# Loading k in token order and packing the shift taps two to a pass, in a convolution-plus-MLP kernel

## The chip, the cores and the metric

The kernel runs on one core of one Trainium2 chip. The metric is the device time of one execution in microseconds (us). Executions of one kernel spread by about one per cent, so every comparison below is of several executions, taken in rounds that alternate a kernel with the kernel before on the same chip. A ratio is the mean time of one kernel's fast executions over that of the other's of the same rounds, so it is not quite the ratio of the medians that are quoted. Each run also leaves one profiled execution, from which all times inside the kernel are read; a difference of about 1 us between two profiled executions is within what one kernel shows twice.

Engines: PE multiplies matrices, DVE and ACT are the two engines that move results out of PSUM ("evacuate" them), Pool is a third element-wise engine, SP only issues DMA transfers. A line such as L317 is a line of that run's kernel; the numbers differ from run to run where lines were added.

## The reference, cut to what matters

```python
def _A_ref(q, k, v, shift_k, ssm_k, ssm_D):        # S = 2048 tokens, D = 512 channels
    k_pad = jnp.pad(k, ((0, 0), (ks - 1, 0), (0, 0)))            # ks = 4 taps
    for t in range(ks):
        k_shift = k_shift + k_pad[:, t:t + S, :] * shift_k[:, ks - 1 - t][None, None, :]
    kv = k_shift * v
    y = ...            # long convolution of kv with ssm_k along the tokens, by FFT
    return q * (y + kv * ssm_D)

def _B_ref(x, w1, b1, w2, b2): ...                  # layer norm, w1, gelu, w2
x = A_q
x = x + _A_ref(_layernorm(x), A_k, ...);  x = x + _B_ref(_layernorm(x), ...)
x = x + _A_ref(_layernorm(x), A_k, ...);  x = x + _B_ref(_layernorm(x), ...)
```

The convolution part of A depends on k, v and the filters alone, so it is computed once. The kernel therefore has a *front* (K = transform of the filter, U = transform of kv, X = second stage of U, T = product of X and K, V and Y = the way back) and then an *MLP stretch* of eight groups, in which the PE is never idle.

## The kernel before: the parts that matter

Work is cut into named pieces. A long string, ORDER, gives their order in the program and for each its engine (`P`, `D`, `A`, `G` Pool, `S` sync) and its buffer. Every engine runs its own pieces strictly in that order.

```python
ORDER = """
warm.P dg0.G lK0.S lK1.S lk1.S lk3.S dg3.G KT0.P0 lk0.S KT1.P1 ... lv0.S lx0.S ... lK2.S
lv1.S ... lH.S ... lk2.S ... lK3.S lM.S ... lW.S ... kv30.P1 ... kv00.P2
# ... (cut)
... Y02.P3 ho.G w1.S w2.S V32.P1 ... TP03.P0 TP13.S pc11.A TP23.S TP03e.D ...
... LT0.P3 gb2.A Y10.P1 Y11.P0 LT0e.D Y10e.A ... Y20.P2 ... LT2.P3 m10x0.P1 ...      # m1.. = MLP
"""
    kT = place([P, CT, NT, KC], 80 * K)                   # KC = 128 + 16
    kd = k_d.rearrange("(p nt) d -> nt p d", nt=NT)       # 16 stripes of 128 tokens
    def ktload(q):                                        # each transposes 128 tokens x 512 channels
        def fn(it):
            for i in range(4 * q, 4 * q + 4):
                nc.sync.dma_start_transpose(kT[:, :, i, 16:16 + P], kd[i])
    # ...
        def diag(it, ct=ct):                              # diagonal matrices of the taps, on Pool
            for t in range(KS):
                nc.gpsimd.tensor_scalar(out=DG[:, ct, t, :], in0=IDt[:], scalar1=sF[:, ct, t:t + 1], ...)
    # ...
            def mms(o, cc=cc, o2=o2):                     # kv: taps of channel chunk cc, token half o2
                for i in range(8):
                    for t in range(KS):
                        tau = 8 * o2 + i - t
                        w = kT[:, cc, tau, 16:16 + P] if tau >= 0 else kT[:, cc, tau + NT, 15:15 + P]
                        nc.tensor.matmul(o[:, i, :], w, DG[:, cc, t, :], start=t == 0, stop=t == KS - 1)
            pe = mm(f"kv{cc}{o2}", 1880, [lk[q] for q in ((0, 1, 3) if o2 == 0 else (1, 2, 3))] + [dg[cc]], mms, [8, P])
            # kvm: uv = taps * v, out of PSUM on DVE; first_stage(...) then makes U from uv
```

Dependences of `kv`: a channel chunk needs three of the four groups of k loads, because each load brings all channels of 128 tokens.

## Time and profile before

| | us |
|---|---|
| median of three executions | 274.45 |
| span of the profiled execution | 271.9 |
| first U product on the PE | 26.1 |
| last V evacuation done | 98.4 |
| first MLP matmul | 113.3 |

The first view is the busy time of each engine in three stretches of before (stretch, its length, then busy us and number of instructions for each engine, the granted PE clock, the DMA share, which can pass 1 as the profile counts it, and GB/s).

```profile
core 0: us, PE busy (x) PEld busy (x) DVE busy (x) ACT busy (x) POOL busy (x), PEclk, DMA share, GB/s
0.00:25.00 25.00, 17.97 (x194) 16.26 (x195) 8.46 (x9) 9.82 (x9) 12.29 (x30) 0.89 0.76 176
25.00:50.00 25.00, 22.84 (x286) 20.40 (x284) 19.17 (x27) 12.77 (x13) 1.24 (x2) 0.91 1.13 297
50.00:90.00 40.00, 37.44 (x541) 33.80 (x539) 38.63 (x41) 37.98 (x41) 0.52 (x1) 1.00 1.00 233
```

DVE and ACT are the engines to look at. In the third stretch they are busy 38.6 and 38.0 of 40 us, so little but less evacuation work could shorten it. In the first two they are busy 27.6 and 22.6 of 50 us: here there is time to win.

What they wait for is in the timeline of the sync queue (start, duration of the issue, line, transfer, count).

```profile
1.72 16.80 SPq L340 DMA_TRANSPOSE arena<-in_A_k_dram  x12
18.57 0.58 SPq L296 DMA_DIRECT2D arena<-in_A_v_dram  x1
...
20.14 0.65 SPq L296 DMA_DIRECT2D arena<-in_A_v_dram  x1
...
21.49 8.06 SPq L340 DMA_TRANSPOSE arena<-in_A_k_dram  x4
...
31.48 0.43 SPq L296 DMA_DIRECT2D Wt<-tabW  x1
```

Twelve transposing loads of k occupy the queue for 16.8 us before v is even asked for; the table W is asked for at 31.5 us. The waits that answer to this are in the list of waits (engine, what it was about to do, what released it, total us, times, longest), of DVE and of the PE:

```profile
DVE arena L422 <- DMA arena<-in_A_v_dram: 9.7, 1, 9.7
```

```profile
PE p_91 L417 <- DMA arena<-in_A_k_dram: 4.4, 4, 1.3
...
PE p_91 L387 <- DMA Wt<-tabW: 2.1, 1, 2.1
```

DVE waited 9.7 us for v before its first multiplication with the taps, the PE 4.4 us in four times for k between the taps, and 2.1 us for W.

The tail before the MLP is in the timeline of all engines, cut to the PE and the sync queue. L507 and L524 finish the first group, L576 transposes its layer norm, L533 are the Y products of later groups and L621 is the first MLP matmul.

```profile
97.76 2.71 SPq L490 DMA_DIRECT2D arena<-in_B_w_dram  x1
...
98.45 0.62 PE L507 MATMUL p_90<-IDt,ZT_77 128*128 128x128 bf16 x8 [1.12 <-ACT ZT_77 L476]
...
100.97 3.43 SPq L512 DMA_TRANSPOSE ZT_83<-ZT_77  x1
...
105.78 1.04 PE L576 MATMUL p_93<-IDt,arena 128*128 128x128 bf16 x8 [5.32 <-DVE arena L268]
...
109.02 1.86 PE L533 MATMUL p_91<-ZT_83,GPt 128*128 128x512 bf16 x4 [2.21 <-issue]
...
113.33 0.93 PE L621 MATMUL p_91<-arena 128*128 128x256 bf16 x7
```

The transpose issued at 100.97 us stands behind the three weight loads (the last at 97.76 us) and its own issue is held up for 3.43 us. The Y product at 109.02 us needed it and the PE had been idle for 2.2 us.

### The profile page before, as it was taken

The page shows a single profiled execution, that of the slowest core. Times are in us where ns is not written, and L with a number is a line of the kernel's source. Part 1 is how long each engine was busy: PE and PEld are TensorE (multiplying, and loading weights), DVE is VectorE, ACT ScalarE, POOL GpSimd, SP SyncE. Part 2 cuts the span into 40 slices and gives each one's busy share as a digit, 9 for nine tenths or more (in the row PEclk, how much of TensorE's full clock was granted, in tenths as well). Part 3 has the DMA queues.
Part 4 walks back from the last instruction along what each step waited for, and adds up shares of the span by engine and source line. Part 5 has one row for each costly group of instructions (what it writes and reads, how often), then busy time and mean ns, then how long its engine had stood idle before and what let it go on. Part 6 is the DMA issues. An engine that isn't in the chain of part 4 may idle for free.

```text
span 271.9 us, 4713 instructions
## 1 busy us (share of the span) xinstructions
PE 243.8 (90%) x1880; PEld 152.6 (56%) x1880; DVE 174.0 (64%) x346; ACT 145.8 (54%) x200; POOL 34.8 (13%) x66
## 2 busy tenths in 40 slices
PE   7839996998999541999999999999999999999994
PEld 7729994996898431595444444444444444444441
DVE  0914875998999899499995987977046920030132
ACT  2650665698999862398475346266704287036000
POOL 3950100000000022103203011111001010000000
PEclk9995997999999995799999999999999999999999
DMA  7949999969899999904034021050210131011111
GB/s 193 128 100 366 270 409 197 218 172 220 315 190 299 168 256 298 172 1 77 4 77 77 2 54 24 0 82 0 49 28 2 39 91 25 2 39 39 39 60 58
DMA packets 62346, 32.89 MB, mean 121 GB/s; under 512 B 57106, under 2 KB 59252, under 8 KB 61172
## 3 DMA queue, kind: packets, MB, share of 16 engines
q1 hardware_dynamic: 61570, 32.52, 50.7%
q8 instruction: 15, 0.25, 0.4%
q10 hardware_dynamic: 674, 0.07, 0.2%
q0 software_dynamic: 80, 0.00, 0.1%
q14 instruction: 7, 0.06, 0.1%
HBM read 12.40 MB, written 2.10 MB: 53 GB/s over the span
## 4 chain that ended last, share of the span: by engine, by line
PE 62%; DMA 12%; SPq 11%; ACT 8%; issue 3%; DVE 3%; DVEq 0%
PE p_93 L643 10%; SPq L340 9%; PE p_90 L643 8%; PE p_91 L621 7%; PE p_90 L621 7%; PE p_92 L621 7%; PE p_93 L621 7%; PE p_92 L643 6%; DMA Wt<-tabW 4%; PE p_91 L643 4%; DMA arena<-in_B_w_dram 4%; DMA ZT_80<-ZT_81 2%; SPq L296 2%; DMA ZT_79<-ZT_78 2%; ACT xb_84 L305 1%
## 5 line engine op out<-in xcount | busy, mean ns | idle before, releaser
L621 PEld LDWEIGHTS <-arena 128*128 128x128 bf16 (+1 forms) x396 | 39.5, 100 | 36.6
L643 PEld LDWEIGHTS <-arena 128*128 128x128 bf16 (+1 forms) x352 | 34.4, 98 | 41.7
L643 PE MATMUL p_93<-arena 128*128 128x512 bf16 (+1 forms) x121 | 27.1, 379 | 0.0
L651 DVE TENSOR_TENSOR arena<-p_93,arena 128x1024 bf16<-128x1024 f32 (+1 forms) x5 | 5.6, 1117 | 30.6 <-PE p_93 L643 30.6
L632 ACT ACTIVATE arena<-p_91,B_72 128x512 bf16<-128x512 f32 (+2 forms) x27 | 15.3, 630 | 16.8 <-PE p_91 L621 8.8
L643 PE MATMUL p_90<-arena 128*128 128x512 bf16 (+1 forms) x99 | 22.2, 379 | 0.0
L632 ACT ACTIVATE arena<-p_90,B_72 128x512 bf16<-128x512 f32 (+3 forms) x26 | 14.9, 639 | 13.3 <-PE p_92 L643 9.8
L621 PE MATMUL p_91<-arena 128*128 128x512 bf16 (+2 forms) x108 | 22.0, 347 | 0.0
L621 PE MATMUL p_90<-arena 128*128 128x512 bf16 (+3 forms) x104 | 21.4, 350 | 0.0
L621 PE MATMUL p_92<-arena 128*128 128x512 bf16 (+2 forms) x96 | 21.0, 361 | 0.0
L417 PEld LDWEIGHTS <-arena 128*128 128x128 bf16 x256 | 17.4, 108 | 5.5 <-DMA arena<-in_A_k_dram 5.3
L621 PE MATMUL p_93<-arena 128*128 128x512 bf16 (+3 forms) x88 | 19.5, 364 | 0.0
L632 ACT ACTIVATE arena<-p_93,B_72 128x512 bf16<-128x512 f32 (+3 forms) x22 | 13.3, 661 | 11.3 <-PE p_93 L621 10.5
L643 PE MATMUL p_92<-arena 128*128 128x512 bf16 (+1 forms) x77 | 17.3, 379 | 0.0
L632 ACT ACTIVATE arena<-p_92,B_72 128x512 bf16<-128x512 f32 (+2 forms) x24 | 14.3, 655 | 4.2 <-PE p_92 L621 3.8
L317 PEld LDWEIGHTS <-arena 128*128 128x128 bf16 x128 | 12.0, 99 | 3.0 <-DVE arena L363 0.7
L417 PE MATMUL p_91<-arena 128*128 128x128 bf16 x128 | 9.4, 234 | 4.4 <-DMA arena<-in_A_k_dram 4.4
L643 PE MATMUL p_91<-arena 128*128 128x512 bf16 (+1 forms) x55 | 12.4, 379 | 0.0
L651 DVE TENSOR_TENSOR arena<-p_90,arena 128x1024 bf16<-128x1024 f32 (+1 forms) x3 | 3.1, 1047 | 14.3 <-PE p_90 L643 14.3
L422 DVE TENSOR_TENSOR arena<-p_91,arena 128x1024 bf16<-128x1024 f32 x4 | 4.9, 1223 | 10.7 <-DMA arena<-in_A_v_dram 9.7
L541 DVE TENSOR_TENSOR arena<-arena 128x1024 bf16<-128x1024 bf16 (+2 forms) x17 | 11.1, 654 | 0.3 <-ACT arena L266 0.3
L250 DVE BATCH_NORM_STATS2 lst_106<-arena 128x6 f32<-128x512 bf16 x16 | 10.3, 685 | 0.1
(193 smaller groups left out, 431.7 us busy)
## 6 DMA issues: line engine op xcount, KB each, us to landing
arena<-arena SPq DMA_DIRECT2D x8, 512.0 KB, 3.9
arena<-in_A_ssm_k_dram SPq DMA_DIRECT2D x4, 512.0 KB, 5.0
arena<-in_A_v_dram SPq DMA_DIRECT2D x2, 1024.0 KB, 7.4
arena<-tabM SPq DMA_DIRECT2D x1, 2048.0 KB, 10.0
arena<-in_A_q_dram SPq DMA_DIRECT2D x1, 1536.0 KB, 8.2
arena<-in_B_w_dram SPq DMA_DIRECT2D x1, 1376.0 KB, 6.8
arena<-in_B_w_dram SPq DMA_DIRECT2D x1, 1280.0 KB, 9.9
Wt<-tabW SPq DMA_DIRECT2D x1, 1024.0 KB, 12.0
```

Of the source, the lines that this page charges most:

```text
L250: nc.vector.bn_stats(self.st[:, i, h, :], xg(g, i, i + 1, c0, c9)[:, 0, :])
L296: return add(name, {"S": 400}, deps, lambda it: nc.sync.dma_start(dst, src), dma=ns, after=after)
L305: nc.scalar.activation(d, s, AF.Copy)
L317: nc.tensor.matmul(o[:, i, :], src[:, 4 * q + i, cs], Ft[:], start=True, stop=True)
L340: nc.sync.dma_start_transpose(kT[:, :, i, 16:16 + P], kd[i])
L417: nc.tensor.matmul(o[:, i, :], w, DG[:, cc, t, :], start=t == 0, stop=t == KS - 1)
L422: nc.vector.tensor_tensor(us, psv(pe, [8, P]), us, ALU.mult)
L541: nc.vector.tensor_tensor(tmpa[:, a:b, c0:c9], ln[:, a:b, c0:c9], ys, ALU.mult)
L621: nc.tensor.matmul(o[0:m, ft - fts[0], :], W1t[:, ct, ft * P:ft * P + m], lnT[n % 3][:, a:b, ct, :], start=ct == 0, stop=ct == CT - 1)
L632: nc.scalar.activation(hT[n % 2][0:m, ft, a * P:b * P], psv(pe, dims)[0:m, ft - fts[0], :], AF.Gelu_apprx_tanh, bias=B1[0:m, ft:ft + 1])
L643: nc.tensor.matmul(o[:, i - a, :], hT[n % 2][0:m, ft, i * P:(i + 1) * P], W2t[0:m, ft, :], start=ft == 0, stop=ft == FT - 1)
L651: nc.vector.tensor_tensor(xs, psv(pe, [2, D])[:, 0:b - a, :], xs, ALU.add)
```

## The change

The intent: fewer transfers ahead of v; tap work in half the PE time; an order of pieces made anew for these costs. The diff, cut to its core:

```diff
-    kT = place([P, CT, NT, KC], 80 * K)
+    kT = place([P, CT, KC], 80 * K)                     # KC = 2048 + 16: tokens in order
-    DG = place([P, CT, KS, P], 114 * K)
+    DG = place([P, CT, KS, RW], 114 * K)                # RW = 64
-    def ktload(q): ... 16 loads, each all channels of 128 tokens
+    def ktload(ct):                                     # 4 loads, each 128 channels of all tokens
+        return lambda it: nc.sync.dma_start_transpose(kT[:, ct, 16:16 + S], k_d[:, ct * P:ct * P + P])
-                nc.gpsimd.tensor_scalar(out=DG[:, ct, t, :], in0=IDt[:], ...)        # 16 of them
+            nc.gpsimd.tensor_tensor(DG[:, ct, :, :], i3, s3, ALU.mult)               # 4 of them
+        def taps(it, cc=cc):
+            tiles = [pf[it["slot"]["ps"]], pf[it["slot"]["ps+"]]]
+            for tau in [0] + list(range(1 - KS, 0)) + list(range(1, NT)):
+                for r in range(RT):                     # two row tiles of 64 channels, RT = 2
+                    # ... first:last = the up to four outputs that source tau feeds, cut at a PSUM bank
+                        w = apf(kT, kT.offset + RW * r * ROW + cc * KC + 16 + tau, [[ROW, RW], [NT, P]])
+                        nc.tensor.matmul(o, w, DG[rows, cc, first - tau:last - tau, :]..., start=bank not in seen, ...)
+        pe = add(f"kv{cc}", {"P": 2400}, [lk[cc], dg], taps, take=["ps", "ps"])
 ORDER (cut)
+warm.P dg.G lK1.S lv1.S lk0.S KT1.P0 KT1e.D lv0.S dt1.D lK0.S ... lk1.S ... kv0.P12 ... lk2.S ... lk3.S
+... V33e.A TP11.S TP03.P0 TP13.S TP03e.D gs0.D Y03.P3 TP33.S Y03e.A pc11.D w1.S Y11.P2
+w2.S gl0.D Y10.P1 Y11e.A TP20.S2 Y30.P0 ... Y31.P3 ... LT0.P2 gb2.D LT0e.A ... LT2.P1 m10x0.P0
```

Each tap matmul now holds one source position of 64 channels as weights and streams the diagonals of up to four taps; the sums of the taps form in PSUM, where each source position adds to up to four outputs.

## The prediction

> **What bounds the kernel now.** The chain of waits shows three stretches.
> (1) 0 to 43.5 us: the load queue. The sync engine issues, one by one, sixteen transposing loads of k (median 1.27 us, 128 KB each, by their source line), then the table loads; the W table lands at 43.5 us and the PE waits 2.1 us for it. In the windows 0 to 50 us DVE is busy 27.6 us and ACT 22.6: together 50 us idle.
> (2) 50 to 90 us: DVE and ACT are busy 38.6 and 38.0 of 40 us. Evacuations bind (f32 128x1024: about 1.14 us apart on DVE, 0.91 on ACT).
> (3) From the last V evacuation (98.4 us) to the first MLP matmul (113.5), 15 us: layer norm, and Y products whose transposes landed at 109 us and later because the weight loads were issued ahead of them. Then the PE runs without a gap at full clock to 268 us.
>
> **What changes.**
> - k: sixteen issues (16 x 1.3 = 21 us of queue) become four of 512 KB. SBUF transposes of that size issue in about 1.8 us: estimate 8 us.
> - Shift taps: 8 groups of 32 matmuls at 1.8 us (14.5 us) become 4 groups of 44 half-height matmuls with up to 256 columns. A 256-column matmul is spaced 0.109 us in the first-stage groups; two tiles side by side give 22 x 0.109 = 2.4 us a group. The Trainium skill (TensorEngine Tiling (Array Packing), Key Properties) says that tiles load and multiply in parallel; this trace doesn't show it. PE is not the limit here, so these 5 us count little. Each group now holds two of four PSUM buffers, which idles ACT.
> - Pool: sixteen scalings (9.3 us) become four broadcast multiplies, estimate 4 us, ending near 12 us. That, or the first k load, releases the first tap group at about 12 us instead of 16 (complete: 24).
> - Evacuations are unchanged. Order: two group-1 and both group-3 Y products and their transposes move ahead of the MLP and the weight loads.
>
> **Sum.** By my queue arithmetic, first U stage at about 17 us (26 before), first U transpose issued near 21 us (38.9), W landed at 35 to 40 us, off the path. By 25 us about 20 us of the 141 us of DVE and ACT work before the last V evacuation is done; the other 121 us plus some 10 us of idle, halved, end at 90 us (98.4): 8 us. Tail: weights start about 3 us after that and land about 8 us after it; layer norm takes 9 to 10 us; the MLP starts about 10.5 us after it, near 101 us (113.5): 4.5 us more. One fewer Y product inside the MLP stretch: 0.9 us. About 13 us off 274.45: **261 us**, 8 in 10 between 255 and 267. Chances: faster by over 2% 0.93, within 2% 0.05, slower 0.02.
>
> **What would show it.** Four k issues near 1.9 us; W landing before 40 us; tap groups near 2.4 us with overlapping matmuls; DVE and ACT over 90% busy from 25 us; last V evacuation near 90 us; first MLP matmul near 101 us; no PE gap after.
>
> **What would make it wrong.** HBM transposes that issue or move slower than the SBUF ones; taps that do not overlap (4.8 us a group); a near-full DMA system that delivers U, swapped K or weights late; a tail bound by the later weight load; a half clock at the MLP's start.

## The result, and the profile after

The median went from 273.67 us (four executions of before) to 260.56 us (259.45 to 260.88); the ratio is 0.9521, interval 0.9457 to 0.9585. In a second group of runs the same kernel (a_same) gave 261.17 us and 0.957 (0.9521 to 0.9618), where 0.95 within 0.006 had been expected. Executions over 1.5% slower than the fastest of the same kernel are left out of the means.

The three stretches again, of after:

```profile
core 0: us, PE busy (x) PEld busy (x) DVE busy (x) ACT busy (x) POOL busy (x), PEclk, DMA share, GB/s
0.00:25.00 25.00, 18.71 (x250) 16.82 (x252) 11.43 (x12) 9.04 (x8) 5.37 (x18) 0.93 1.06 238
25.00:50.00 25.00, 23.89 (x287) 20.29 (x282) 24.92 (x35) 19.95 (x20) 1.24 (x2) 1.00 1.10 259
50.00:90.00 40.00, 31.39 (x475) 28.62 (x473) 35.80 (x43) 35.42 (x39) 2.53 (x3) 1.00 1.09 245
```

DVE and ACT now do 20.5 us of work by 25 us (18.3 before) and 44.9 us between 25 and 50 us (31.9 before). Between 50 and 90 us they are *less* dense than before (71.2 of 80 us against 76.6).

The sync queue of after:

```profile
1.25 0.42 SPq L306 DMA_DIRECT2D arena<-in_A_v_dram  x1
1.73 6.45 SPq L347 DMA_TRANSPOSE arena<-in_A_k_dram  x1
8.22 0.57 SPq L306 DMA_DIRECT2D arena<-in_A_v_dram  x1
...
9.31 12.06 SPq L347 DMA_TRANSPOSE arena<-in_A_k_dram  x3
...
22.82 7.82 SPq L456 DMA_TRANSPOSE ZT_78<-ZT_77  x2
...
31.35 0.44 SPq L306 DMA_DIRECT2D Wt<-tabW  x1
```

The four k loads hold the queue for 6.45 and 12.06 us, 18.5 us together: a quarter less than the 24.9 us (16.80 and 8.06) of the sixteen for the same 2 MB, and W is asked for no earlier (31.35 us, 31.48 before). But half of v goes first and the rest of it at 8.2 us, so the long DVE wait for v is gone. In its place DVE waits 5.1 us for the taps, and those 2.6 us for the first k load; the last line is for the tail below:

```profile
DVE arena L448 <- PE p_91 L434: 5.1, 1, 5.1
```

```profile
PE p_90 L434 <- DMA arena<-in_A_k_dram: 2.6, 1, 2.6
...
PE p_89 L658 <- ACT arena L315: 1.2, 1, 1.2
```

The taps themselves, in the timeline of the PE (the columns after the line are operation, PSUM tile and source, shape in 64 rows by columns):

```profile
12.90 0.41 PE L434 MATMUL p_90<-arena 64*128 64x256 bf16 x1
12.91 0.41 PE L434 MATMUL p_91<-arena 64*128 64x256 bf16 x1
13.11 0.41 PE L434 MATMUL p_90<-arena 64*128 64x256 bf16 x1
...
21.71 0.27 PE L434 MATMUL p_91<-arena 64*128 64x256 bf16 x1
21.73 0.27 PE L434 MATMUL p_92<-arena 64*128 64x256 bf16 x1
21.82 0.27 PE L434 MATMUL p_91<-arena 64*128 64x256 bf16 x1
```

The two row tiles start up to 20 ns apart, at the timeline's resolution of 10 ns, and run side by side. A pair takes 0.21 us in the first group and 0.11 us in the second: the PE had been waiting before the first, and its clock had dropped. The page's row of granted clock shows the same gap (40 slices, tenths of full speed), the 3rd slice is 13 to 19.4 us:

```profile
PEclk9979999999999959999999999999999999999999
```

A group takes 3.5 us at that clock and 1.97 us at full speed. The tail of after (L542 and L561 finish the first group, L570 are Y products, L658 the first MLP matmul):

```profile
89.70 0.62 PE L542 MATMUL p_89<-IDt,ZT_81 128*128 128x128 bf16 x8 [1.83 <-ACT ZT_81 L511]
...
90.25 1.29 SPq L549 DMA_TRANSPOSE ZT_77<-ZT_81  x1
...
91.59 1.33 SPq L549 DMA_TRANSPOSE ZT_82<-ZT_81  x1
...
93.02 0.53 SPq L306 DMA_DIRECT2D arena<-in_B_w_dram  x1
...
93.76 1.86 PE L570 MATMUL p_91<-ZT_77,GPt 128*128 128x512 bf16 x4 [1.67 <-DMA ZT_77<-ZT_81]
...
101.53 1.91 PE L658 MATMUL p_89<-arena 128*128 128x256 bf16 x16 [1.19 <-ACT arena L315]
```

The transposes that the Y products need are issued ahead of the weights, at 90.25 and 91.59 us, and the products run from 93.76 us.

### The profile page after: what moved, and what is told of

It is laid out like the page before. It is cut to its first block, busy times and chain, and to the rows that moved or that the text cites. A ratio compares the mean times of both kernels' runs of the same rounds, so it can differ in the third digit from the quotient of the medians.

```text
span 259.2 us, 4520 instructions
## 1 busy us (share of the span) xinstructions
PE 236.0 (91%) x1800; PEld 144.2 (56%) x1800; DVE 172.0 (66%) x347; ACT 145.5 (56%) x199; POOL 28.3 (11%) x54
## 4 chain that ended last, share of the span: by engine, by line
PE 69%; DMA 12%; DVE 8%; ACT 6%; issue 2%; SPq 1%; POOL 0%; ACTq 0%; DVEq 0%; POOLq 0%
PE p_89 L680 10%; PE p_92 L680 8%; PE p_91 L658 8%; PE p_92 L658 8%; PE p_89 L658 7%; PE p_90 L658 7%; PE p_90 L680 6%; PE p_91 L680 5%; DMA arena<-in_A_k_dram 4%; DMA ZT_78<-ZT_76 3%; DMA arena<-arena 2%; ACT arena L315 2%; DMA ZT_82<-ZT_81 2%; DVE arena L317 2%; DVE arena L448 2%
## 5 line engine op out<-in xcount | busy, mean ns | idle before, releaser
L658 PEld LDWEIGHTS <-arena 128*128 128x128 bf16 (+1 forms) x396 | 39.6, 100 | 37.9 <-issue 1.3
L680 PE MATMUL p_89<-arena 128*128 128x512 bf16 (+1 forms) x121 | 27.1, 379 | 0.0
L669 ACT ACTIVATE arena<-p_91,B_71 128x512 bf16<-128x512 f32 (+3 forms) x26 | 15.8, 663 | 18.5 <-PE p_92 L680 9.8
L658 PE MATMUL p_91<-arena 128*128 128x512 bf16 (+3 forms) x104 | 23.3, 367 | 0.0
L658 PE MATMUL p_92<-arena 128*128 128x512 bf16 (+3 forms) x108 | 22.4, 351 | 0.0
L680 PE MATMUL p_92<-arena 128*128 128x512 bf16 (+1 forms) x99 | 22.2, 379 | 0.0
L669 ACT ACTIVATE arena<-p_92,B_71 128x512 bf16<-128x512 f32 (+3 forms) x27 | 15.5, 632 | 11.8 <-PE p_92 L658 11.7
L658 PE MATMUL p_89<-arena 128*128 128x512 bf16 (+1 forms) x96 | 18.9, 343 | 1.2 <-ACT arena L315 1.2
L669 ACT ACTIVATE arena<-p_89,B_71 128x512 bf16<-128x512 f32 (+1 forms) x24 | 13.2, 613 | 12.0 <-PE p_90 L680 7.8
L658 PE MATMUL p_90<-arena 128*128 128x512 bf16 (+2 forms) x88 | 19.2, 360 | 0.0
L680 PE MATMUL p_90<-arena 128*128 128x512 bf16 (+1 forms) x77 | 17.3, 379 | 0.0
L327 PEld LDWEIGHTS <-arena 128*128 128x128 bf16 x128 | 11.9, 97 | 6.4 <-issue 2.0
L669 ACT ACTIVATE arena<-p_90,B_71 128x512 bf16<-128x512 f32 (+2 forms) x22 | 13.1, 645 | 4.0 <-PE p_90 L658 2.3
L680 PE MATMUL p_91<-arena 128*128 128x512 bf16 (+1 forms) x55 | 12.4, 379 | 0.0
L315 ACT ACTIVATE arena<-p_92 128x2048 bf16<-128x2048 bf16 (+2 forms) x6 | 7.0, 1166 | 8.6 <-PE p_92 L383 6.1
L434 PEld LDWEIGHTS <-arena 64*128 64x128 bf16 x176 | 8.9, 149 | 3.6 <-DMA arena<-in_A_k_dram 2.9
L257 DVE BATCH_NORM_STATS2 lst_105<-arena 128x6 f32<-128x512 bf16 x16 | 10.3, 684 | 0.6 <-DMA arena<-in_A_q_dram 0.5
L257 DVE BATCH_NORM_STATS2 lst_97<-arena 128x6 f32<-128x512 bf16 x16 | 10.2, 682 | 0.0
```

The costliest lines, as they stand in the source:

```text
L257: nc.vector.bn_stats(self.st[:, i, h, :], xg(g, i, i + 1, c0, c9)[:, 0, :])
L315: nc.scalar.activation(d, s, AF.Copy)
L327: nc.tensor.matmul(o[:, i, :], src[:, 4 * q + i, cs], Ft[:], start=True, stop=True)
L434: nc.tensor.matmul(o, w, DG[rows, cc, first - tau:last - tau, :].rearrange("p t c -> p (t c)"), start=bank not in seen, stop=tau == NT - 1 ...
L658: nc.tensor.matmul(o[0:m, ft - fts[0], :], W1t[:, ct, ft * P:ft * P + m], lnT[n % 3][:, a:b, ct, :], start=ct == 0, stop=ct == CT - 1)
L669: nc.scalar.activation(hT[n % 2][0:m, ft, a * P:b * P], psv(pe, dims)[0:m, ft - fts[0], :], AF.Gelu_apprx_tanh, bias=B1[0:m, ft:ft + 1])
```

## Experiments

Two rival theories about the front stood against my own. **A** (mine): the loads open the front earlier and the denser order fills it; the PE time of the taps hardly counts. **B**: the taps are the gain. **C**: the order of pieces alone is the gain, whatever the loads. A further theory, **D**, is about waits that remain. Twelve kernels were run, all correct, eleven of them altered.

The table gives, from each profiled execution, the time of the first U product, the end of the last V evacuation, and the first MLP matmul; then the median and the ratio to before with its interval.

| run | first U | last V | MLP | median us | ratio to before |
|---|---|---|---|---|---|
| before | 26.1 | 98.4 | 113.3 | 274.45 | 1 |
| after | 18.5 | 89.7 | 101.5 | 260.56 | 0.952 (0.946-0.959) |
| b_fourloads | 21.8 | 96.9 | 112.1 | 272.74 | 0.997 (0.993-1.002) |
| a_fulltaps | 22.5 | 94.7 | 105.2 | 266.29 | 0.973 (0.969-0.977) |
| a_sixteen | 34.1 | 102.6 | 115.1 | 274.41 | 1.003 (0.999-1.006) |
| b_tpfirst | 25.4 | 97.1 | 109.4 | 270.91 | 0.991 (0.988-0.995) |
| a_same | 19.5 | 89.5 | 101.6 | 261.17 | 0.957 (0.952-0.962) |
| a_serialtaps | 23.4 | 95.2 | 106.7 | 266.33 | 0.976 (0.970-0.981) |
| a_early | 17.4 | 87.8 | 100.1 | 259.06 | 0.948 (0.943-0.953) |
| a_wfirst | 19.2 | 89.1 | 109.9 | 268.96 | 0.984 (0.979-0.989) |
| a_early2 | 18.3 | 89.3 | 100.9 | 260.21 | 0.953 (0.950-0.957) |
| a_sw | 18.8 | 90.0 | 101.2 | 258.80 | 0.947 (0.942-0.951) |
| a_all | 15.9 | 88.3 | 99.3 | 258.64 | 0.947 (0.943-0.951) |
| a_vhalf | 14.8 | 89.0 | 99.9 | 260.25 | 0.953 (0.949-0.957) |

From the first MLP matmul to the end of the span there are 157.7 us in after and 158.6 in before. A run's letter says which of the two kernels was altered. The runs stand in four groups on the same chip each: b_fourloads to b_tpfirst, a_same to a_wfirst, a_early2 to a_all, and a_vhalf alone.

### b_fourloads: the loads alone

```diff
 in before:
+    kT = place([P, CT, KC], 80 * K);  four loads lk0..lk3 as in after, at the old places in ORDER
-    w = kT[:, cc, tau, 16:16 + P] if tau >= 0 else kT[:, cc, tau + NT, 15:15 + P]
+    w = apf(kT, kT.offset + cc * KC + 16 + tau, [[ROW, P], [NT, P]])
-    ... [lk[q] for q in ((0, 1, 3) if o2 == 0 else (1, 2, 3))] + [dg[cc]]
+    ... [lk[cc], dg[cc]]
```

> The kernel before with one part of the change: k in token order by four transposing loads of 512 KB; full-height taps, scalings on the Pool engine and the old order of pieces stay. Theory A (k loads open the front: the loads' place in the sync queue held back v, U and the W table): 3 to 6 us faster than before, W landing at 35 to 39 us instead of 43.5, first U stage before 22 us instead of 26. Theory B (the gain is the tiled taps) and theory C (the gain is the order alone): within 1 us of before.

Measured: 0.9974, no gain to speak of. The expectation of theory A failed. The first U product did come earlier, at 21.8 us, within what was expected. The queue did get shorter: the four loads hold it for 21.0 us in place of 24.9, and W was asked for at 27.7 us:

```profile
1.73 13.24 SPq L337 DMA_TRANSPOSE arena<-in_A_k_dram  x3
...
18.04 7.77 SPq L337 DMA_TRANSPOSE arena<-in_A_k_dram  x1
```

But three k loads held the sync queue until 15.0 us, and the old order puts the taps of the third chunk early and its load (lk2) late: issued at 18.0 us behind v, it landed at 29.2 us, and the PE waited for it in the middle of the front. The waits of this run's PE show it (the second line is the first U product, which waits for DVE's multiplication of v with the taps):

```profile
PE p L413 <- DMA arena<-in_A_k_dram: 2.9, 2, 2.1
PE p L317 <- DVE arena L418: 2.0, 1, 2.0
```

From the first U product to the last V evacuation this run took 75.1 us, against 72.3 in before: most of the early start was lost on the way. New loads under an order made for the old ones are worth almost nothing.

### a_sixteen: the new order on the old loads

```diff
 in after:
-    four loads, kT = place([P, CT, KC], ...)
+    the sixteen loads and kT = place([P, CT, NT, KC], ...) of before
-    ... {"P": 2400}, [lk[cc], dg]
+    ... {"P": 2400}, lk + [dg]
-    lo = 16 + tau
+    lo = tau % NT * KC + (16 if tau >= 0 else 15)
```

> The kernel after with the sixteen old k loads put back, in the old layout, at the places of the four; tiled taps and new order stay (two of the loads' places had to be written ahead of the first tap group, the sync queue's own order is the same). Theory A: the first tap group waits for all sixteen, to about 24 to 27 us instead of 12.4; 8 to 12 us slower than after. Theory C (order alone): within 2 us of after.

Measured: 1.0026 of before, so 12.5 us above after (0.0456 of 274). The PE's waits:

```profile
PE p L438 <- DMA arena<-in_A_k_dram: 15.8, 3, 13.5
```

The first tap group waits in all 15.8 us for k. Its end moves to 31.2 us, the first U product to 34.1 us. Theory C is refuted for this order: order and tiled taps without the loads gain nothing. Every tap group of this run needs all sixteen loads; before's own taps, which need twelve, were not tried in an order made anew with v ahead of the loads, so how much of the gain that alone would bring stays open. Together with b_fourloads this is the main finding: the loads without the rest of the change, and the rest without the loads, move the time by less than 1 us each, both together by 13.

The two runs also show how the front behaves as a whole. From the first U product to the last V evacuation, before, after and all other runs but three take 70 to 72.5 us, a_sixteen 68.5. What sets the end of the front is mostly when it starts. Only b_fourloads and a_vhalf (75.1 and 74.2 us) lose on the way.

### a_fulltaps and a_serialtaps: the taps

```diff
 a_fulltaps, in after: tiles and diagonals of full height again
+            for h in range(2):
+                for i in range(8):
+                    for t in range(KS):
+                        w = apf(kT, kT.offset + cc * KC + 16 + 8 * h + i - t, [[ROW, P], [NT, P]])
+                        nc.tensor.matmul(tiles[h][:, P * i:P * i + P], w, DG[:, cc, t, :], start=t == 0, stop=t == KS - 1)
```

> The kernel after with the tiled taps undone: 64 full-height 128-column matmuls a group in place of 44 half-height ones; loads and order as after. Theory A (PE time is not the limit): tap groups go from 2.0 to about 3.6 us at full clock, 6.5 us more PE work, but only 1 to 3 us more in total, from the first groups that lie on the chain. Theory B (the taps are the gain): 6 to 10 us more.

Measured: 0.973. Against after's two measurements (0.952 and 0.957) that is 4.4 to 5.7 us more, above what theory A had expected and below theory B. One thing looked unclean in this run: the wider diagonals took Pool longer (4.0 us in place of 2.3), and the first tap group started at 13.7 us, 1.2 us later than in after, waiting for Pool. The later start is not due to the edit, though: Pool began late because the shift table landed late (12.6 us), and a_same, which is after unchanged, started as late for the same reason. The first line is of a_fulltaps, the second of a_same:

```profile
13.68 6.34 PE L418 MATMUL p<-arena 128*128 128x128 bf16 x64 [4.18 <-POOL arena L405]
...
13.69 3.26 PE L434 MATMUL p<-arena 64*128 64x256 bf16 x44 [3.84 <-POOL arena L410]
```

A second run kept everything of after, the same matmuls and the same Pool work, and only changed their sequence:

```diff
 a_serialtaps, in after
-            for tau in [0] + list(range(1 - KS, 0)) + list(range(1, NT)):
-                for r in range(RT):
+            for r in range(RT):
+                for tau in [0] + list(range(1 - KS, 0)) + list(range(1, NT)):
```

> The kernel after with the same tap matmuls, but all of one row tile ahead of all of the other, so that neighbours lie in the same rows of the array. Theory A1 (the pairs run side by side, and the first groups lie on the chain): a group takes 4.0 to 4.5 us at full clock instead of 2.0 and the total grows by 3 to 5 us, as with full-height taps. Theory A2 (what mattered in the full-height run was its later scalings on Pool and not the taps): within 1.5 us of after.

Its tap groups in the PE's timeline (44 matmuls a group; the second line is the K transposes behind the first group, the third is two groups):

```profile
13.54 6.54 PE L434 MATMUL p<-arena 64*128 64x256 bf16 x44 [1.96 <-DMA arena<-in_A_k_dram]
20.01 3.59 PE L383 MATMUL p<-IDt,ZT 128*128 128x128 bf16 x32
...
26.66 7.15 PE L434 MATMUL p<-arena 64*128 64x256 bf16 x88
...
51.92 3.79 PE L434 MATMUL p<-arena 64*128 64x256 bf16 x44
```

A group takes 6.5 us at half clock and 3.6 to 3.8 at full, against 3.5 and 1.97 when the two tiles alternate. So the tiles do run side by side, and a pair that lies in the same rows does not. The ratio is 0.9756 against 0.957 of after in the same group of runs: 5.1 us (0.0186 of 274, each ratio known to half a per cent) are due to the changed sequence alone. Against a_same, whose first tap group started at nearly the same time (13.69 us), the first U product is 3.9 us later and the last V evacuation 5.7 us. Three of those microseconds are the first group, which everything waits for; it runs at half clock, where the overlap is worth double. In this execution half speed lasted longer than in after, from 8 us at the latest to about 24 us: the 32 K transposes took 3.59 us, against 1.96 in a_same, which is clock and not overlap. How much of the 5.1 us is of this kind one trace can't tell; a_fulltaps, whose K transposes took 1.95 us, agrees with its 4.4 to 5.7 us. (The trace records a granted clock of 1.00 there; that it was half is read from the durations: 16 first-stage matmuls of K took 3.60 us, against 1.92 in a_same.) The second and third groups lie back to back and hold all four PSUM buffers, so that ACT has nothing to evacuate (its waits for the first-stage products grow): these two groups took 7.15 us in place of 3.9, another 3 us, of which 1.8 reach the last V evacuation. The fourth, in the middle of a dense stretch, hides. Theory A's "the taps hardly count" is refuted in its size, and theory B as the whole story. The four broadcast multiplies on Pool in place of sixteen scalings were not tested alone.

### b_tpfirst and a_wfirst: the tail

```diff
 b_tpfirst, in before
-... Y02.P3 ho.G w1.S w2.S V32.P1 ... TP13.S pc11.A TP23.S TP03e.D
+... Y02.P3 ho.G V32.P1 ...           TP13.S pc11.A TP23.S w1.S w2.S TP03e.D
 a_wfirst, in after
-... V33e.A TP11.S TP03.P0 TP13.S ... TP33.S Y03e.A pc11.D w1.S Y11.P2 w2.S
+... V33e.A TP11.S w1.S w2.S TP03.P0 TP13.S ... TP33.S Y03e.A pc11.D Y11.P2
```

> The kernel before with only the tail's order changed: the last-chunk transposes of groups 1 and 2 are issued ahead of the two weight loads. Theory A (the MLP's start at 113.5 us was held by Y products that waited for transposes behind the weights): MLP starts at 108 to 110 us, 3 to 5 us faster in total. Rival (the tail is set by the layer norm chain or by the weights' landing): within 1 us of before.

Measured: 0.9912, or 2.4 us, a little under the expected 3 to 5. The MLP started at 109.4 us as expected, but 1.3 us of that came from an earlier front in this execution. From the last V evacuation to the MLP there are 12.3 us against 14.9 in before, 2.6 us, which agrees with the time.

> The kernel after with the two weight loads issued ahead of the last-chunk transposes of groups 1 and 3, as before had it. Theory A (the tail's gain comes from those transposes going first): the Y products wait, the MLP starts 4 to 7 us later and the total grows by as much. Rival (the layer norm chain and its queue on ACT set the MLP's start): within 1 us of after.

Measured: 0.9837 against 0.957 of after in the same group, 7.3 us more, just above the range. One wait explains it:

```profile
PE p L570 <- DMA ZT<-ZT: 10.0, 1, 10.0
```

The Y products of two groups, which after puts ahead of the MLP, wait 10 us for transposes behind the weights, and the MLP starts 20.9 us after the last V evacuation in place of 11.9. The rival, that layer norm sets the start, is refuted for this order. So Y products ahead of the MLP pay only if their transposes are ahead of the weights; the transposes alone, without more Y products, were worth 2.4 us (b_tpfirst).

### a_early, a_early2, a_vhalf: starting earlier still

In after the first tap group waits for two things that come at about 12 us: the first k load, behind 1 MB of v, and Pool's diagonals, whose shift table was third on its queue and landed at 11.4 us.

```diff
 a_early, in after                       a_early2: F table, shift table, Dc in that order
+    nc.scalar.dma_start(sT[:], ...)      # ahead of the F table and Dc
     nc.scalar.dma_start(Ft[:], ...)
-... lK1.S lv1.S lk0.S KT1.P0
+... lK1.S lk0.S lv1.S KT1.P0             # in both
```

> The kernel after with the shift table first on its queue and the first k load ahead of the first v load. Theory A (the start of the first tap group lies on the chain): first tap group at 8.5 to 10 us instead of 12.4, at a higher clock, and the total falls by 1.5 to 3 us. Rival (the DMA system, near full from 10 to 90 us, sets the end of the front, so that an earlier start is lost again): within 0.7 us of after.

Measured: 0.9479 against 0.957 of after in the same group, 2.5 us less; the executions of the two (258.27 to 259.41 and 260.96 to 262.4 us) don't overlap. The means failed in a detail: the first tap group started at 12.3 us and not at 8.5 to 10, because the first stage of K now waited 3.3 us for the F table. But the group ran at full clock in 2 us and not 3.5; the half clock fell on the first stage of K, which took 3.2 us in place of 1.9. Mending the F table was the next run.

> As the earlier-start run, but with the F table first on its queue, then the shift table, so that the first stage of K no longer waits 3.3 us for F. Theory A (start of the first tap group on the chain): first tap group at 8.5 to 10.5 us, the total 1 to 2 us below the earlier-start run and 3 to 4 below after. Rival (from here on the near-full DMA system or the v loads set the pace): the first V product is not waiting for the taps any more, and the total stays within 0.7 us of the earlier-start run.

Measured: 0.9534, not better than a_early (0.9479, another chip). The taps did start earlier, at 9.7 us. Then:

```profile
DVE arena L448 <- DMA arena<-in_A_v_dram: 5.2, 1, 5.2
```

```profile
PE p L327 <- DVE arena L448: 5.0, 2, 4.5
```

DVE waits 5.2 us for v, the PE with it, and the PE's clock drops again (the first twelve U matmuls take 2.74 us, 1.48 in a_same). In this execution the rival, that the v loads set the pace from here on, holds. It is not so in each: a_all below has its loads in the same order, and there DVE did not wait for v at all; it started on v at 13.5 us, where here v landed at 15.7. With that in doubt, v was loaded by channel halves in the last run, on top of a_all below:

```diff
 a_vhalf, in a_all
-    lv = [load(f"lv{o}", uv[:, 8 * o:8 * o + 8, :], vd[:, 8 * o:8 * o + 8, :], 2650) for o in range(2)]
+    lv = [load(f"lv{o}", uv[:, :, 256 * (1 - o):256 * (2 - o)], vd[:, :, 256 * (1 - o):256 * (2 - o)], 2650) for o in range(2)]
-    ... {"D": 1140}, [pe] + lv, mul ...
+    ... {"D": 1140}, [pe, lv[1 - cc // 2]], mul ...
-... lv0.S dt1.D lK0.S K1S0.P1 lk1.S
+... dt1.D lK0.S K1S0.P1 lk1.S lv0.S
```

> The combined version with v also loaded by channel halves (256 channels of all tokens each, 1 MB) in place of token halves, the second half behind the second k load; so the first U stage needs 2 MB of loads (one K part, one k part, half of v) instead of 3.5 MB. Theory A extended (the front opens when the bytes that the first channel chunk needs have landed): first U stage at 14 to 16 us instead of 18.5 and 2 to 4 us below the combined version. Rival (from 10 to 90 us the DMA system as a whole, near full, sets the pace, so that an earlier first chunk is lost again): within 0.7 us of the combined version.

Measured: 0.9531, not faster than a_all (0.9467, another chip). The first U product came at 14.8 us as expected, and yet the last V evacuation at 89.0 us: 74.2 us for the front in place of 72.4 in a_all. The start was lost again by 25 us: DVE and ACT had done 21.4 us of work by then, 24.7 in a_all. Later transfers are seen to hold it up: the PE waited 2.9 us for a later chunk's k load, to 22.7 us, a wait that a_all's trace does not list, ran those taps at half clock (3.4 us), and waited another 1.3 us for a part of K, as in a_all. The DMA share is 1.06 to 1.10 in all three stretches. The gain that the extended theory A expected is absent. Whether the two kernels are within 0.7 us, as the rival expected, can't be told between two chips (the ratios are 1.8 us apart and their intervals overlap), and that the DMA system as a whole is the limit was not shown.

### a_sw and a_all

```diff
 a_sw, in after
-... K210.P2 U3T0.S1 K213.P3 ...  X11.P2 sw10.S X02e.A2
+... K210.P2 K213.P3 ...          X11.P2 sw10.S U3T0.S1 X02e.A2
 a_all: a_early2, a_sw, and
-... LT0.P2 gb2.D LT0e.A
+... LT0.P2 gb2.D LT0e.D
```

> The kernel after with the last swap of K issued ahead of the first U3 transpose in the sync queue. Theory D (some of the DVE and ACT idle between 50 and 90 us comes from single transfers that sit in the queue behind blocked issues): the wait of 1.4 us of a K product for the swap vanishes and the total falls by 0.5 to 1.5 us. Rival (the DMA system as a whole is the limit there): within 0.5 us of after.

Measured: 0.9469, against 0.952 and 0.957 of after in other groups. DVE's wait of 1.4 us for the swapped K is gone, as expected; DVE waits 1.6 us for ACT instead in that place, and the last V evacuation is no earlier (90.0 us) in the profiled execution. With fast executions from 257.1 to 260.5 us (one at 260.98 counts as slow) a gain of 1 us can't be told from none. Inconclusive.

> Both together, and the first transposed layer norm half evacuated on DVE in place of ACT, where it stood behind four Y evacuations. Expected if each is worth what theories A and D say: 4 to 6 us below after, the MLP starting 0.9 us earlier against the last V evacuation; a version faster than both kernels.

Measured: 0.9467, median 258.64 us of all five (fast executions 257.49 to 258.64; the ratio leaves the two slow ones out). About 2 us under after, not the 4 to 6 expected. Evacuating the first layer norm half on DVE did what was expected: from the last V evacuation to the MLP 11.0 us in place of 11.9. All three of a_early, a_sw and a_all beat both kernels by their medians; for a_early this was shown in one group of runs.

## Why the prediction was right, point by point

The predicted time was 261 us and the measured one 260.56 us. The chain of effects held; that the number fits to half a microsecond is partly luck, because errors in it cancel. The sum and the profiled executions:

| term | predicted | measured (before and after) |
|---|---|---|
| last V evacuation | 98.4 to 90: 8.4 us | 98.4 to 89.7: 8.7 us |
| from there to the MLP | 15 to 10.5: 4.5 us | 14.9 to 11.9: 3.1 us |
| MLP stretch, one Y product fewer | 0.9 us | 158.6 to 157.7: 0.9 us |

- **The front.** Right: first tap group at 12.4 us ("about 12"), 20.5 us of evacuation work done by 25 us ("about 20"), last V evacuation at 89.7 us ("90"). DVE was 93% busy from 25 to 90 us and ACT 85%, where over 90% had been named for both; idle of the two was 13.9 us, not 10. That it still came out rests on a second error: "evacuations are unchanged" counted 141 us of work for DVE and ACT ahead of the last V evacuation, and after did 136.3 (before 140.3), because part of the layer norm had moved: ACT's normalisation of x (2.9 us) is gone and DVE does one of 1.5 us, with fewer statistics. Some 5 us less work and some 4 us more idle cancelled. The first U product came at 18.5 us ("about 17"), the first U transpose at 22.8 ("21").
- **The k loads.** The step "SBUF transposes of that size issue in about 1.8 us: estimate 8 us" failed: the four issues took 18.5 us. The trace of before already spoke against it: its eight SBUF transposes of that size took 1.7 to 5.1 us to issue, and 1.8 was the low end. It did no harm because v was placed ahead of most of them. What the new loads bring is not mainly a shorter queue: b_fourloads had a shorter one and gained nothing clear of noise. A channel chunk's taps need one load of 512 KB, where before they needed twelve of 128 KB (for half of the tokens). That this opens the front only with an order that uses it is shown by b_fourloads (0.997) and a_sixteen (1.003).
- **Pool.** The four multiplies took 2.3 us, not 4, but began only at 11.4 us, when the shift table landed. The first tap group was released by the k load at 12.4 us, shortly after Pool's first multiply: the time was right, and the cost and start of the Pool work were not.
- **The taps.** Side by side as predicted, and shorter: 1.97 us, because I had counted all 22 pairs as 256 columns wide, while they sum to 16 times 256. The step "PE is not the limit here, so these 5 us count little" failed: a_serialtaps shows that undoing the overlap costs 5.1 us, a part of which can be its longer half clock. At the start of a front the evacuating engines are idle *because* they wait for the PE.
- **The tail.** The cause was right (b_tpfirst, a_wfirst), the size 1.4 us too large: the MLP waited 1.2 us for ACT, which had four Y evacuations ahead of the layer norm half (a_all).
- **W.** The PE used it at 39.4 us without waiting, as predicted, but not by the shorter queue of the prediction: it was asked for at 31.35 us as before (31.48), and had landed within 8.1 us, where it took 12.0 us in before.

The parts don't add up: taken out of after one by one, loads, overlap and tail order cost 12.5, 5.1 and 7.3 us (12.5 across two groups of runs), 25 us in all, for a gain of 13. An order of pieces fits the costs that it was made for.

## What to carry to other kernels

Ask of a load not how long the queue is busy with it but which first piece of work it completes; then make the order of pieces anew, and judge the two together. An engine with time to spare still sets the pace where the busy engines have nothing to do yet, so shorten what stands before the *first* evacuation. When the first start has been pulled forward, look at the next transfer before pulling further: here a first U product at 14.8 us (a_vhalf) in place of 15.9 (a_all) bought nothing.

## What the Trainium skill lacked or had wrong

- "DMA: Bandwidth & Descriptors", section "Issuing engines are not separate DMA queues", calls the time to initiate a DMA "usually small relative to the DMA itself". For transposing transfers with others in flight it was not: the four k loads of after held the sync queue 2.4 to 6.6 us each, of 5.9 to 10.7 us from issue to landing. No run here shows what the issue waits for.
- "TensorE: Matmul & The Clock Gate", closing table "Why this matters for your kernels", gives starts at most 4 ns apart for row tiles (its row on small-K matmuls). The timeline, with a resolution of 10 ns, shows 0 to 20 ns. What it says of the overlap agrees: 0.11 us for a pair of 256 columns; and a group takes 3.6 us in place of 1.97 when neighbours lie in the same rows.
- The same table asks for no idle gaps over about 3 us between bursts. In after a gap of 2.6 us ahead of the first tap group came with half clock behind it (0.21 us a pair, 3.5 us a group), and in a_all a gap of 1.97 us ahead of the first stage of K did too (3.20 us for 16 matmuls, 1.92 in a_same after a gap of 1.57). A limit that is safe for one gap can't be read from these runs.
- "TensorEngine Tiling (Array Packing)", "Key Properties", says that a change of tiling mode drains the PE, and gives no cost. In after the first full-height matmul starts 0.19 us after the last tap pair at half clock (15.73 to 15.92 us) and 0.13 us at full clock (46.00 to 46.13 us), where pairs of 64 columns otherwise start 0.07 and 0.04 us apart. About 0.1 us a change is left, an estimate from these starts; whether it is the drain was not shown.
